# RWKV-5 attention with a SiLU MLP on one core: k turned by DMA in two 16-bit planes from unit 10 on

## The chip, the core and the metric

One core of a Trainium2 chip runs the kernel. Its engines are TensorE (PE in the profile, PEld for its weight loads), VectorE (DVE), ScalarE (ACT), GpSimd (POOL) and SyncE (SP), which here only issues DMAs. Each engine runs its own list of instructions in order and waits on semaphores. The metric is the device time of one execution in microseconds, the median of several runs.

## What is computed

For each of 4 batches and 8 heads a state of 48 x 48 runs over 768 steps, and the result goes through an MLP:

```python
for t in range(S):
    cur = np.einsum('bhd,bhe->bhde', u[None] * kt, vt)
    y[:, :, t] = np.einsum('bhd,bhde->bhe', rt, state + cur)
    state = w[None, :, :, None] * state + np.einsum('bhd,bhe->bhde', kt, vt)
...
h = x @ w_in                       # x: 3072 x 384, w_in: 384 x 2048
g = h * (1.0 / (1.0 + np.exp(-h)))
return (g @ w_out)                 # w_out: 2048 x 384
```

Inputs and output are f32.

## The kernel before

The sequence is cut into 6 chunks of 128 steps. A unit is one chunk of one batch with all 8 heads: unit i is chunk i//4 of batch i%4, 24 in all. Units 0 to 5 are done in an order written out by hand (the string `order`); the loop at L686 takes the others in pairs, i = 6, 8, ..., 22, where b = i%4 is 2 or 0. Tiles hold the time step on partitions, except for those that end in T, which hold the head's 48 channels there, two heads beside each other (partitions 0 to 47 and 64 to 111), in 4 groups.

A chunk is treated as two halves of 64 steps. Within a half the products of r and k are weighted by powers of w: r by w^t (`lamR`), k by w^-(t+1) (`lamK`). A pair i goes through these steps, each an engine's work:

- `sums` (L418, PE): k (weighted to the end of its half, `kc`, f16) times v, per half, into PSUM `sp`; `state_first` and `state_second` (L435, L449, DVE) add them to the decayed state (`sdec`, `st`). `spread_state` copies the state to f16 for the outputs (`s1h` on ACT, `s0h` on POOL and ACT).
- `product_halves` (L395, PE): kT times rT into PSUM `att`; `masked_halves` (L402, DVE) masks it into `am`.
- `outputs_halves` (L492, L501, PE): r times state and `am` times v into `yp`; `evict_halves` (L343, DVE) adds the bonus `vu` and gives `y16`; `turn_y_dma` (L524) turns y16 to `xT` by DMA transpose on SP's queue, one DMA for each unit.
- For the next pair (`nxt`, units i+2 and i+3): `bonus_products` (L223, L228, POOL) and `decayed_k` (L231, POOL, `kc`), `bonus_sum` (L236, DVE), `bonus_v` (L241, POOL), `cast_v` (L246, ACT, `v16`), `turn` (L255, PE: r and k of a unit turned in 64x64 blocks against an identity, 8 matmuls each, into `att`), `decay` (L270, DVE: rT and kT, times lamR and lamK), `decay_r16` (L270 and `rX`: the crossed halves of r in f16, on DVE or, where b=0, on ACT at L289).
- `load` (L72, SP): r, k, v of units i+4 and i+5, as r k v r k v, into rings of 8 buffers.

Between these, `fill(n)` takes n steps of the MLP from a list: an l1 step is 3 matmuls of 512 columns (L546) with xT as the moving operand and a SiLU on ACT (L555, `gT`); an l2 step is 4 matmuls (L568) with gT as weights, and each fourth of them ends a unit's output, which ACT copies to `osb` (L574) and SP stores (L578). A chunk has 16 of each. PSUM has four shared buffers (tag `moe`) for sp, yp, hps and ops, so a matmul that opens a new one waits until the engine that reads the oldest is done with it.

Of the kernel before, what the change touches and what calls it, by code (L numbers as in the profile page):

```python
# [7 lines left out]

FP = mybir.dt.float32
F16 = mybir.dt.float16  # L10
AF = mybir.ActivationFunctionType
ALU = mybir.AluOpType

# [2 lines left out]
def kernel(  # L16
# [33 lines left out]
    def unit(i):  # L50
        return divmod(i, B)
# [46 lines left out]

    RZ = 96
    w_row = cst.tile([RZ + 1, HD], FP)  # L100
    u_row = cst.tile([RZ + 1, HD], FP)
    ones = cst.tile([RZ + 1, 128], FP)
    idle = cst.tile([128, 512], F16)
    nc.scalar.preload_act_table_set("natural_log_exp_and_others")
# [6 lines left out]
    it_row = cst.tile([PR, 2, C], FP)  # L111
    it_rev = cst.tile([128, 1], FP)
    it_half = cst.tile([128, 1], FP)
    maskM = cst.tile([128, C], FP)
    maskH = cst.tile([128, HC], FP)
    ident16 = cst.tile([128, 128], F16)
    carry_pairs = [big.tile([PR, 2, NP, PW], F16, name=f"s0p{n}") for n in range(2)]
    inner_pairs = [big.tile([PR, 2, NP, PW], F16, name=f"s1p{n}") for n in range(2)]
    carry = [big.tile([D, 2, H, D], F16, name=f"s0h{n}") for n in range(3)]
    inner = [big.tile([PR, 2, H, D], F16, name=f"s1h{n}") for n in range(2)]  # L120

# [4 lines left out]
    def column_numbers():  # L126
        nc.gpsimd.iota(it_rev, pattern=[[0, 1]], base=C - 1, channel_multiplier=-1,
                       allow_small_or_imprecise_dtypes=True)
        for y in range(2):
            nc.gpsimd.iota(it_half[HC * y:HC * y + HC], pattern=[[0, 1]], base=HC - 1,  # L130
                           channel_multiplier=-1, allow_small_or_imprecise_dtypes=True)

    def mask():
# [17 lines left out]
    lnw_bc = cst.tile([128, HD], FP)  # L151
    lamC = cst.tile([128, H, D], FP)
    lamH = cst.tile([128, H, D], FP)
    wHT = cst.tile([PR, NP], FP)

    def pad(i, eng=nc.vector):
        for dst in (rin, kin):
# [32 lines left out]
    def spread_row(name, src):  # L190
        spread[name] = ps.tile([128, HD], FP, name="bc", tag="moe", bufs=4)
        nc.tensor.matmul(spread[name], ones, src, start=True, stop=True)
# [11 lines left out]
    def powers_h():  # L204
        nc.scalar.activation(out=lamH.rearrange("p h d -> p (h d)"), in_=lnw_bc,
                             func=AF.Exp, scale=it_half)
        nc.scalar.activation(out=wHT, in_=lnwT, func=AF.Exp, scale=float(HC))

    def silu_table():
        nc.scalar.preload_act_table_set("silu_and_others")  # L210

# [2 lines left out]
    def L(i):  # L214
        return live.setdefault(i, {})
# [14 lines left out]
    def decayed_k(i, eng=nc.gpsimd):  # L230
        eng.tensor_tensor(out=kc[i % NIN][:, :, 0:D], in0=kin[i % NIN][:, :, 0:D],  # L231
                          in1=lamH if in_halves(i) else lamC, op=ALU.mult)
# [8 lines left out]
        eng.tensor_tensor(out=L(i)["vu"], in0=vin[i % NIN],  # L241
                          in1=L(i)["rku"].unsqueeze(2).broadcast_to([128, H, D]), op=ALU.mult)

    def cast_v(i):
        L(i)["v16"] = wrk.tile([128, H, D], F16, name="v16", bufs=4)
        nc.scalar.copy(out=L(i)["v16"], in_=vin[i % NIN])  # L246

    def turn_one(i, x):
        if x == 0:
            L(i)["t"] = next_att().rearrange("p y (x g t) -> p y x g t", x=2, g=NP)  # L250
        flat = (rin, kin)[x][i % NIN].rearrange("p h d -> p (h d)")
        for p in range(NP):
            for y in range(2):
                rows = slice(HC * y, HC * y + HC)
                nc.tensor.transpose(L(i)["t"][0:PR, y, x, p, :], flat[rows, 128 * p:128 * p + PR],  # L255
                                    ident[rows, rows])
# [3 lines left out]

    def decay_one(i, x, key=None):
        lam = (lamR, lamK)[x]
        if key is None:
            key = "rk"[x] + "T"
            L(i)[key] = wrk.tile([PR, NP, C], FP, name=key)
        else:
            L(i)[key] = wrk.tile([PR, NP, C], F16, name=key, bufs=4)
        lam = (lam[:, :, 0:HC].unsqueeze(1).broadcast_to([PR, 2, NP, HC]) if in_halves(i)
               else lam.rearrange("p g (y t) -> p y g t", y=2))
        nc.vector.tensor_tensor(  # L270
            out=L(i)[key].rearrange("p g (y t) -> p y g t", y=2),
            in0=L(i)["t"][0:PR, :, x], in1=lam, op=ALU.mult)

    def early(i):
        return unit(i)[0] < 2
# [4 lines left out]
    def decay_r16(i, by_vector):  # L280
        decay_one(i, 0, "rT16")
        rx = L(i)["rX16"] = wrk.tile([PR, NP, HC], F16, name="rX16", bufs=4)
        for x in range(2):
            here, there = crossed_rows(x)
            if by_vector:
                nc.vector.tensor_tensor(out=rx[here], in0=L(i)["t"][there, x, 0],
                                        in1=lamR[there, :, 0:HC], op=ALU.mult)
            else:
                nc.scalar.copy(out=rx[here], in_=L(i)["rT16"][there, :, HC * x:HC * x + HC])  # L289

# [3 lines left out]

    def turn(i):
        turn_one(i, 0)
        turn_one(i, 1)

    def decay(i):
        decay_one(i, 0)  # L300
# [42 lines left out]
        nc.vector.tensor_tensor(out=y16[a], in0=y[b, 0:HD], in1=vu[a], op=ALU.add)  # L343

    def new_y(i):
        L(i)["y16"] = wrk.tile([128, H, D], F16, name="y16", bufs=4)

    def evict_first(i):
        new_y(i)
# [57 lines left out]
    def sums(i):  # L407
        sc, b = unit(i)
        xs = range(2 if sc < NCH - 1 else 1)
        L(i)["sp"] = [ps.tile([128, 512], FP, name="sp", tag="moe", bufs=4) for _ in xs]  # L410
        for p in range(NP):
            for e in range(2):
                for x in xs:
                    rows = slice(HC * x, HC * x + HC)
                    for j in range(2):
                        h = 2 * p + j
                        c0 = (e * NP + p) * D
                        nc.tensor.matmul(L(i)["sp"][x][64 * j:64 * j + 64, c0:c0 + D],  # L418
                                         kc[(i + e) % NIN][rows, h, :],
                                         L(i + e)["v16"][rows, h, :],  # L420
                                         start=True, stop=True)
# [94 lines left out]

    def x_tile(sc):
        if sc not in xts:
            xts[sc] = wrk.tile([128, NQ, B, C], F16, name="xT", bufs=2)
        return xts[sc]  # L520

    def turn_y_dma(i):
        sc, b = unit(i)
        nc.sync.dma_start_transpose(out=x_tile(sc)[:, :, b, :],  # L524
                                    in_=L(i)["y16"].rearrange("p h d -> p (h d)"))

    def turn_y(i):
        yf = L(i)["y16"].rearrange("p h d -> p (h d)")
# [3 lines left out]

    def copy_x(i, copy=nc.scalar.copy):
        sc, b = unit(i)
        copy(out=x_tile(sc)[:, :, b, :], in_=L(i)["yT"])

    gts = {}

# [2 lines left out]
    def l1_mm(sc, b0, nb, ft):  # L541
        m = B // nb
        hps = hpss[b0, ft] = ps.tile([128, m, nb * C], FP, name="hps", tag="moe", bufs=4)
        for f in range(m):
            for q in range(NQ):
                nc.tensor.matmul(hps[:, f, :], win[(ft + f) // 4].rearrange("p q (t c) -> p q t c", c=4)  # L546
                                 [:, q, :, (ft + f) % 4],
                                 xts[sc][:, q, b0:b0 + nb, :].rearrange("p b t -> p (b t)"),
                                 start=(q == 0), stop=(q == NQ - 1))

    def l1_silu(sc, b0, nb, ft):
# [76 lines left out]
    def piece(word, f):  # L628
# [7 lines left out]
        "wr": lambda: row(w_row, w), "wx": lambda: columns(nc.sync, wpT, w, 1),  # L636
        "wy": lambda: columns(nc.scalar, wpT, w, 0), "lnw": powers_r, "eK": exponents_k,
        "lamK": powers_k, "uc": copy_u, "wb": lambda: spread_row("w", w_row),
        "ub": lambda: spread_row("u", u_row), "lnwb": ln_w, "lamC": powers_c, "lamH": powers_h,
        "tab": silu_table, "clear": clear, "spin": lambda: None, "H": lambda: halved.pop(0)(),  # L640
    }
    unit_steps = {
# [16 lines left out]
        id16 lr1 pd3 lr3 lk3 clear 6*spin lv0 cg0 lv1 kz7 lr2 ak2 ku0 lv3 lr5 kz2 lv2 ub pd1 lv4  # L659
        lr4 lk4 lv5 pd2 lk5 lk7 lr6 lk6 uc T0 1*spin T1 lr7 lv7 kT0 pa4 rT0 ru0 ku1  # L660
        v160 pd5 lv6 rT1 kz6 rd0 kT1 wb ru1 P0 n0 2*spin rd1 P1 vu0 lnwb T2 n1 v161 2*spin
        pd7 lamC lamH pa6 i_q0 V0 v162 tab rT2 e0 kT2 ku2 T3 1*spin yT0 V1 kz5 vu1 i_q1 ru2
        xTD0 e1 P2 yT1 kT3 rd2 rT3 ku3 xTD1 P3 ru3 n2 rd3 v163 n3 L0.0 vu2 kc0 1*spin G0.0
        vu3 V2 L0.2 V3 G0.2 L0.4 e2 i_q2 e3 kc1 yT2 yT3 S0 G0.4 xT2 xTD3 kc2 L0.6 L2.4 G0.6
        st0 L2.0 scA0 v164 kc3 L2.6 ku4 i_q3 v165 L2.2 T4 rT4 kT4 G2.4 ru4 G2.2 T5 G2.0 G2.6
# [17 lines left out]
            unit_steps[word[:-1]](int(word[-1]))  # L683
    fillers.extend(halved + begun)

    for i in range(B + 2, NU, 2):  # L686
        sc, b = unit(i)
        nxt = range(i + 2, min(i + 4, NU))
        sums(i)
        product_halves(i)  # L690
        state_first(i)
        state_second(i)
        masked_halves(i)
        if i == B + 2:
            bonus_sum(i + 1)
            bonus_v(i + 1)
        for n in nxt:
            bonus_products(n)
            decayed_k(n)
        if i > B + 2 or sc < NCH - 1:  # L700
            next_state(i)
        fill(4)
        outputs_halves(i)
        next_crossed(i)
        for n in nxt:
            turn(n)
        evict_halves(i)
        turn_y_dma(i)
        turn_y_dma(i + 1)
        if b:  # L710
            fillers.extend((first(sc) if sc > 1 else rest_first(sc)) + second(sc))
        for n in nxt:
            decay(n)
        load(i + B)
        load(i + 1 + B)
        fill(4)
        for n in nxt:
            bonus_sum(n)
            cast_v(n)
            bonus_v(n)  # L720
        for n in nxt:
            fill(2)
            decay_r16(n, b)
        fill(4 if i < NU - 4 else 2)
    fill(len(fillers))


# [28 lines left out]
```

## Time and profile before

| | us |
|---|---|
| median of 3 runs | 187.34 (186.94 to 188.56) |
| the profiled execution | 186.19 |
| its span, first to last instruction | 184.5 |
| DMA queue of SP (q1), share of 16 engines | 50.3% |
| granted clock of TensorE | 0.998 |

The span is what the profile covers; the rest of the execution's time lies around it. A row of the profile names line, engine, operation, and output <- inputs; a matmul's own length in such rows overlaps its neighbours', so the cost of a run of them is read from the chain of waits, where each piece is counted until the next begins. A number in square brackets is idle time ahead of an instruction, with what ended it. "SPq" is the time for which SP's sequencer issued a DMA; the data land later.

### The profile page before, as it was taken

What the parts mean: (1) busy time and instruction counts of PE and PEld (TensorE: products, weight loads), DVE (VectorE), ACT (ScalarE), POOL (GpSimd) and SP (SyncE); (2) the same over time, 40 slices, a digit from 0 to 9 for tenths busy, and PEclk for the clock granted to TensorE, in tenths of its full rate; (3) what the DMA queues carried; (4) which work ended last, traced back from release to release, by engine and by line L of the source; (5) the groups of instructions that cost most, each with busy time, mean ns of one, the idle gap of its engine ahead of it and who ended that gap; (6) DMA issues with size and microseconds to landing.
All of it is one profiled execution on the core that took longest, in us unless ns stands there. A gap on an engine that the chain in (4) does not pass through costs nothing.

```text
span 184.5 us, 6822 instructions
## 1 busy us (share of the span) xinstructions
PE 177.5 (96%) x2913; PEld 117.2 (64%) x2913; DVE 115.9 (63%) x226; ACT 106.8 (58%) x209; POOL 112.1 (61%) x148
## 2 busy tenths in 40 slices
PE   7987998999999999999999999999999999999993
PEld 2565785688666976756657656657656566555563
DVE  4799729786885855895845985946974954000120
ACT  3462788599124694268694268694377692299200
POOL 7999999997999439639558567579169030000000
PEclk9999999999999999999999999999999999999999
DMA  5999999899596386386295396293396201410022
GB/s 95 235 211 210 167 216 195 151 221 230 100 190 198 89 168 138 87 171 174 46 176 130 87 182 163 48 217 88 87 187 159 46 4 49 125 43 0 0 88 85
DMA packets 88594, 24.24 MB, mean 131 GB/s; under 512 B 83314, under 2 KB 88052, under 8 KB 88564
## 3 DMA queue, kind: packets, MB, share of 16 engines
q1 hardware_dynamic: 83952, 20.19, 50.3%
q0 software_dynamic: 2176, 3.15, 10.2%
q10 hardware_dynamic: 2436, 0.46, 1.3%
q8 instruction: 23, 0.38, 0.8%
q14 instruction: 7, 0.06, 0.1%
HBM read 20.45 MB, written 4.72 MB: 136 GB/s over the span
## 4 chain that ended last, share of the span: by engine, by line
PE 73%; POOL 17%; DMA 6%; issue 2%; ACT 0%; POOLq 0%
PE ops L568 33%; PE hps L546 26%; DMA kin<-in_k_dram 6%; PE att L395 4%; PE att L255 4%; POOL ku L223 4%; POOL kc L231 3%; POOL rku_f L228 3%; POOL vu L241 2%; PE yp L492 2%; PE sp L418 2%; PE ops L593 1%; POOL win L83 1%; PE yp L501 1%; POOL wout L88 1%
## 5 line engine op out<-in xcount | busy, mean ns | idle before, releaser
L546 PE MATMUL hps<-xT,win 128*128 128x512 f16 (+1 forms) x360 | 66.3, 337 | 0.3 <-DMA win<-in_moe_w_in_dram 0.3
L555 ACT ACTIVATE gT<-hps 128x512 f16<-128x512 f32 x96 | 56.0, 597 | 14.1 <-PE hps L546 10.6
L568 PE MATMUL ops<-wout,gT 128*128 128x384 f16 x368 | 62.5, 326 | 0.0
L546 PEld LDWEIGHTS <-win 128*128 128x128 f16 x360 | 38.9, 114 | 21.3 <-DMA win<-in_moe_w_in_dram 0.4
L568 PEld LDWEIGHTS <-gT 128*128 128x128 f16 x368 | 35.2, 98 | 23.3
L241 POOL TENSOR_TENSOR vu<-vin,rku 128x384 f32<-128x384 f32 x24 | 19.6, 831 | 22.7 <-DVE rku L236 22.6
L223 POOL TENSOR_TENSOR ku<-kin,rin 128x384 f32<-128x384 f32 x24 | 24.1, 1003 | 11.6 <-DMA kin<-in_k_dram 11.5
L270 DVE TENSOR_TENSOR rT<-att,lamR 112x512 f32<-112x512 f32 (+1 forms) x40 | 26.9, 682 | 4.2 <-PE att L255 3.8
L574 ACT COPY osb<-ops 128x384 f32<-128x384 f32 x20 | 9.6, 479 | 34.1 <-issue 18.1
L343 DVE TENSOR_TENSOR y<-yp,vu 64x384 f16<-64x384 f32 (+1 forms) x34 | 18.9, 555 | 16.1 <-PE yp L501 8.0
L228 POOL TENSOR_TENSOR rku_f<-ku,u_bc 128x384 f32<-128x384 f32 x24 | 24.1, 1003 | 1.5
L231 POOL TENSOR_TENSOR kc<-kin,lamH 128x384 f16<-128x384 f32 x20 | 20.1, 1007 | 0.0
L270 DVE TENSOR_TENSOR kT<-att,lamK 112x512 f32<-112x512 f32 x24 | 16.3, 681 | 0.1
L246 ACT CAST v<-vin 128x384 f16<-128x384 f32 x24 | 11.3, 510 | 7.8 <-DMA vin<-in_v_dram 7.5
L435 DVE TENSOR_TENSOR s<-sp,sdec 112x384 f32<-112x384 f32 x10 | 5.6, 558 | 16.1 <-PE sp L418 16.1
L576 DVE COPY osb<-ops 128x384 f32<-128x384 f32 x3 | 1.7, 558 | 21.3 <-PE ops L568 21.3
L402 DVE TENSOR_TENSOR am<-att,maskH 128x1024 f16<-128x1024 f32 x10 | 12.2, 1219 | 1.1 <-PE att L395 1.1
L236 DVE TENSOR_REDUCE rku<-rku_f 128x8 f32<-128x384 f32 x24 | 12.4, 543 | 0.0
L395 PE MATMUL att<-rT,kT 48*64 48x64 f32 x640 | 11.9, 220 | 0.5 <-issue 0.5
L374 ACT CAST s1h<-s 48x384 f16<-48x384 f32 x16 | 8.1, 509 | 5.4 <-DVE s L435 5.2
L395 PEld LDWEIGHTS att<-rT,kT 48*64 48x64 f32 x640 | 10.6, 135 | 0.7 <-issue 0.7
L255 PE MATMUL att<-ident,rin 64*112 64x64 f32 x192 | 10.0, 223 | 0.4 <-DVE rku L236 0.4
(92 smaller groups left out, 175.0 us busy)
## 6 DMA issues: line engine op xcount, KB each, us to landing
rin<-in_r_dram SPq DMA_DIRECT2D x24, 192.0 KB, 3.9
vin<-in_v_dram SPq DMA_DIRECT2D x24, 192.0 KB, 4.3
out_dram<-osb SPq DMA_DIRECT2D x23, 192.0 KB, 2.7
kin<-in_k_dram SPq DMA_DIRECT2D x22, 192.0 KB, 4.5
win<-in_moe_w_in_dram POOLq DMA_DIRECT2D x4, 384.0 KB, 6.0
wout<-in_moe_w_out_dram POOLq DMA_DIRECT2D x4, 384.0 KB, 6.7
kin<-in_k_dram ACTq DMA_DIRECT2D x2, 192.0 KB, 3.7
xT<-y SPq DMA_TRANSPOSE x18, 2.3
```

The costliest lines, as they stand in the source:

```text
L223: eng.tensor_tensor(out=L(i)["ku"], in0=kin[i % NIN][:, :, 0:D], in1=rin[i % NIN][:, :, 0:D], op=ALU.mult)
L228: eng.tensor_tensor(out=L(i)["rku_f"], in0=L(i)["ku"], in1=u_bc, op=ALU.mult)
L231: eng.tensor_tensor(out=kc[i % NIN][:, :, 0:D], in0=kin[i % NIN][:, :, 0:D], in1=lamH if in_halves(i) else lamC, op=ALU.mult)
L236: nc.vector.tensor_reduce(out=L(i)["rku"], in_=L(i)["rku_f"], axis=mybir.AxisListType.X, op=ALU.add)
L241: eng.tensor_tensor(out=L(i)["vu"], in0=vin[i % NIN], in1=L(i)["rku"].unsqueeze(2).broadcast_to([128, H, D]), op=ALU.mult)
L255: nc.tensor.transpose(L(i)["t"][0:PR, y, x, p, :], flat[rows, 128 * p:128 * p + PR], ident[rows, rows])
L270: nc.vector.tensor_tensor(out=L(i)[key].rearrange("p g (y t) -> p y g t", y=2), in0=L(i)["t"][0:PR, :, x], in1=lam, op=ALU.mult)
L343: nc.vector.tensor_tensor(out=y16[a], in0=y[b, 0:HD], in1=vu[a], op=ALU.add)
L395: nc.tensor.matmul(a[o0:o0 + HC, j, e, p, :], kT[r0:r0 + D, p, HC * x:HC * x + HC], rT[r0:r0 + D, p, HC * x:HC * x + HC], start=True, stop ...
L546: nc.tensor.matmul(hps[:, f, :], win[(ft + f) // 4].rearrange("p q (t c) -> p q t c", c=4) [:, q, :, (ft + f) % 4], xts[sc][:, q, b0:b0 + ...
L555: nc.scalar.activation(out=gts[sc][:, ft:ft + m, b0 * C:(b0 + nb) * C], in_=hpss[b0, ft], func=AF.Silu)
L568: nc.tensor.matmul(opss[b], gts[sc][:, ft, b * C:(b + 1) * C], wout[:, ft, :], start=(ft == 0), stop=(ft == NFT - 1))
```

## The change

From unit 10 on (`by_planes`: i > 9) k is no longer turned on PE. POOL weights k by the channel's power of w relative to the middle of its half (`lamN`) into an f32 tile `kd`; a copy splits the f32 words of two units into their low and high 16-bit halves (`planes`, 128 x 2 x 2 x 8 x 64, zero in the padding); one DMA transpose on SP's queue turns both units' planes, 16 blocks of 128 x 128, into `turned`; and a copy on ACT joins the halves to f32 words again, `kT`. The sums' operand `kc` is now a cast of kd, on ACT where b=2 and on POOL where b=0, and v16 goes with it. r is weighted from the middle too (`lamS`, `lamM`), and the state is rescaled once, on POOL in i=6 and i=8, and then kept in that scale. `weighted_k` and `split_k` are done for units i+4 and i+5 in iteration i, right behind their loads, which now come as k k r r v v; the first split (units 10, 11) is on ACT in i=8. `masked_halves` moves ahead of `state_second`; `rX` is on DVE in every iteration; the two y16 of a pair lie in one tile and are turned by one DMA (6 blocks), for which xT has the unit ahead of the 128-channel block; the number of l2 steps ahead of the outputs is 3 for 4 where b=2.

```diff
+    it_mid = cst.tile([128, 1], FP)
-    carry_pairs = [big.tile([PR, 2, NP, PW], F16, name=f"s0p{n}") for n in range(2)]
-    inner_pairs = [big.tile([PR, 2, NP, PW], F16, name=f"s1p{n}") for n in range(2)]
+    blocks16 = big.tile([128, 8 * NP * PW], F16)
...
+    kd = [lnw_bc, u_wide]
+    lamM = lamR[:, :, HC // 2:HC // 2 + HC]
+    turned = blocks16[:, 0:16 * C].bitcast(U16).rearrange("p (e y g t) -> p e y g t", e=2, y=2, t=C)
+    lamN = cst.tile([128, H, D], FP)
+    lamS = cst.tile([PR, NP, HC], FP)
+    planes = big.tile([128, 2, 2, H, 64], U16)
...
+    def powers_n():
+        nc.scalar.activation(out=lamN.rearrange("p h d -> p (h d)"), in_=lnw_bc,
+                             func=AF.Exp, scale=it_mid)
...
     def decay_one(i, x, key=None):
         lam = (lamR, lamK)[x]
+        if by_planes(i):
+            lam = lamS if key is None else lamM
...
+    def clear_planes():
+        nc.gpsimd.memset(planes.rearrange("p e y h d -> p (e y h d)").bitcast(F16), 0.0)
+
+    def by_planes(i):
+        return i > 2 * B + 1
+
+    def powers_s():
+        nc.gpsimd.tensor_tensor(out=lamS, in0=lamR[:, :, 0:HC],
+                                in1=lamK[:, :, HC // 2 - 1:HC // 2].broadcast_to([PR, NP, HC]), op=ALU.mult)
+
+    def rescale_state(i):
+        t = st[unit(i)[1] // 2]
+        nc.gpsimd.tensor_tensor(
+            out=t, in0=t, in1=lamK[:, :, HC // 2 - 1:HC // 2].unsqueeze(1).broadcast_to([PR, 2, NP, D]),
+            op=ALU.mult)
+
+    def cast_k(i, copy=nc.scalar.copy):
+        copy(out=kc[i % NIN][:, :, 0:D], in_=kd[i % 2].rearrange("p (h d) -> p h d", h=H))
+
+    def weighted_k(i):
+        nc.gpsimd.tensor_tensor(out=kd[i % 2].rearrange("p (h d) -> p h d", h=H), in0=kin[i % NIN][:, :, 0:D], in1=lamN, op=ALU.mult)
+
+    def split_k(i, copy=nc.gpsimd.tensor_copy):
+        copy(out=planes[:, i % 2, :, :, 0:D],
+             in_=kd[i % 2].bitcast(U16).rearrange("p (h d y) -> p y h d", h=H, y=2))
+
+    def turn_planes():
+        nc.sync.dma_start_transpose(out=turned.rearrange("p e y g t -> p (e y g) t"),
+                                    in_=planes.rearrange("p e y h d -> p (e y h d)"))
+
+    def join_k(i):
+        L(i)["kT"] = wrk.tile([PR, NP, C], FP, name="kT")
+        nc.scalar.copy(
+            out=L(i)["kT"].rearrange("p g t -> p (g t)").bitcast(U16)
+            .rearrange("p (n y) -> p n y", y=2),
+            in_=turned[0:PR, i % 2].rearrange("p y g t -> p (g t) y"))
...
     def turn(i):
         turn_one(i, 0)
-        turn_one(i, 1)
+        if not by_planes(i):
+            turn_one(i, 1)
...
-            xts[sc] = wrk.tile([128, NQ, B, C], F16, name="xT", bufs=2)
+            xts[sc] = wrk.tile([128, B, NQ, C], F16, name="xT", bufs=2)
...
-        nc.sync.dma_start_transpose(out=x_tile(sc)[:, :, b, :],
-                                    in_=L(i)["y16"].rearrange("p h d -> p (h d)"))
+        nc.sync.dma_start_transpose(out=x_tile(sc)[:, b:b + 2].rearrange("p b q t -> p (b q) t"),
+                                    in_=L(i)["yy"].rearrange("p e h d -> p (e h d)"))
...
-                                 xts[sc][:, q, b0:b0 + nb, :].rearrange("p b t -> p (b t)"),
+                                 xts[sc][:, b0:b0 + nb, q, :],
...
+    clear_planes()
+    powers_s()
     for i in range(B + 2, NU, 2):
         sc, b = unit(i)
         nxt = range(i + 2, min(i + 4, NU))
+        after = range(i + 4, min(i + 6, NU))
+        split = i + 2 < NU and by_planes(i + 2)
         sums(i)
         product_halves(i)
         state_first(i)
+        masked_halves(i)
         state_second(i)
-        masked_halves(i)
+        if by_planes(i + 4) and not by_planes(i):
+            rescale_state(i)
         if i == B + 2:
             bonus_sum(i + 1)
             bonus_v(i + 1)
+        if i == 2 * B:
+            for n in nxt:
+                split_k(n, nc.scalar.copy)
+        if split:
+            turn_planes()
+        if b and split:
+            for n in nxt:
+                cast_k(n)
+                cast_v(n)
         for n in nxt:
             bonus_products(n)
-            decayed_k(n)
+            if not split:
+                decayed_k(n)
         if i > B + 2 or sc < NCH - 1:
             next_state(i)
-        fill(4)
+        if not b and split:
+            for n in nxt:
+                cast_k(n, nc.gpsimd.tensor_copy)
+                cast_v(n, nc.gpsimd.tensor_copy)
+        fill(3 if b and split else 4)
         outputs_halves(i)
         next_crossed(i)
         for n in nxt:
             turn(n)
         evict_halves(i)
         turn_y_dma(i)
-        turn_y_dma(i + 1)
         if b:
             fillers.extend((first(sc) if sc > 1 else rest_first(sc)) + second(sc))
         for n in nxt:
-            decay(n)
-        load(i + B)
-        load(i + 1 + B)
+            if split:
+                decay_one(n, 0)
+                if b:
+                    join_k(n)
+            else:
+                decay(n)
+        for dst, src in ((kin, k), (rin, r), (vin, v)):
+            for n in after:
+                ld(n, dst, src)
         fill(4)
+        if i > 2 * B and not b and split:
+            for n in nxt:
+                join_k(n)
         for n in nxt:
             bonus_sum(n)
-            cast_v(n)
+            if not split:
+                cast_v(n)
             bonus_v(n)
+        for n in after:
+            weighted_k(n)
+        if after and by_planes(i + 4) and not i == B + 2:
+            for n in after:
+                split_k(n)
         for n in nxt:
             fill(2)
-            decay_r16(n, b)
-        fill(4 if i < NU - 4 else 2)
+            decay_r16(n, True)
+        if i == 2 * B and split:
+            for n in nxt:
+                join_k(n)
+        fill((5 if b and split else 4) if i < NU - 4 else 2)
```

## The prediction

> **What bounds it now.** I read the page's busy shares first, then the chain of waits in order of time, then the timelines of SP, ACT and POOL in one iteration.
>
> ```profile
> PE 177.5 (96%) x2913; PEld 117.2 (64%) x2913; DVE 115.9 (63%) x226; ACT 106.8 (58%) x209; POOL 112.1 (61%) x148
> 83.29 0.37 PE sp L418 x32
> 83.66 0.98 PE att L395 x63
> 84.64 2.71 PE hps L546 x12
> 87.36 0.37 PE yp L492 x32
> 87.73 0.28 PE yp L501 x32
> 88.01 1.04 PE att L255 x32
> 89.05 4.66 PE hps L546 x21
> 93.70 3.25 PE ops L568 x20
> 96.95 0.37 PE sp L418 x32
> ```
>
> Columns are start, length, what. This is all of the iteration i=12, 13.66 us, and each piece starts where the one before ends: from 47.6 us to the end the chain is TensorE alone. So an instruction taken off PE there is worth its time, as long as nothing else comes late. I write +x for x us after an iteration's first sums matmul.
>
> SP's queue, ACT, and rows of POOL and ACT by form:
>
> ```profile
> 88.71 2.48 SPq L524 DMA_TRANSPOSE xT<-y  x2
> 91.28 0.53 SPq L72 DMA_DIRECT2D rin<-in_r_dram  x1
> 91.91 0.53 SPq L72 DMA_DIRECT2D kin<-in_k_dram  x1
> ```
>
> ```profile
> 89.85 2.54 ACT L555 ACTIVATE gT<-hps 128x512 f16<-128x512 f32 x4 [1.47 <-PE hps L546]
> 92.42 0.93 ACT L246 CAST v<-vin 128x384 f16<-128x384 f32 x2
> ...
> 95.19 0.60 ACT L555 ACTIVATE gT<-hps 128x512 f16<-128x512 f32 x1
> ```
>
> ```profile
> L228 POOL TENSOR_TENSOR rku_f<-ku,u_bc 128x384 f32<-128x384 f32 x24 | 24.1, 1003 | 1.5
> ...
> L374 POOL CAST s0h<-st 48x384 f16<-48x384 f32 x8 | 4.0, 499 | 0.0
> ```
>
> ```profile
> L289 ACT COPY rX<-rT 48x256 f16<-48x256 f16 x16 | 6.4, 403 | 0.3
> ```
>
> The first fence shows SP issuing: one DMA transpose of 3 blocks of 128x128 holds the queue 1.2 us, a load 0.53. The gT lines show how little room ScalarE has: the last gT ends at 95.79 and the l2 matmul that needs it comes 15 x 0.1625 us (3.25/20) after 93.70, at 96.14: 0.35 us of slack. The last two are prices (busy us, mean ns).
>
> **Removed from PE.** In iterations 8, 10, ..., 20 the 16 k transposes of two units: half of the 1.04 us, 0.52 x 7 = 3.64 us. The iteration becomes 13.1 us. The two kT products on DVE go too (2 x 0.68); DVE takes rX back where b=0 (4 x 0.42). It waited 1.1 to 3.0 us for the sums each time, so this ends on no path. am moves ahead of the four st updates: PE gets am 1 us sooner, st comes 1.2 us later, and its readers on POOL stand behind 4 us of bonus products.
>
> **xT in another order.** The l1 matmuls read four runs of 128 in place of one of 512. No row has that. 42 matmuls of 256 columns took 4.71 us (112 ns), 21 of 512 took 4.66 (222 ns): a joint costs 2 ns at most, three joints in 192 matmuls at most 1.3 us; I take 0, as the price goes by columns; a gain is excluded, since no column is saved.
>
> **The transpose of the planes.** 16 blocks a pair. The trace has 3 blocks in 1.2 us of queue. Bounds: 1.2 us (all fixed) and 16/3 x 1.2 = 6.4 (all by blocks). I take a load's 0.53 as the fixed part, (1.2 - 0.53)/3 = 0.22 a block: P = 4.0 us, and 1.8 for the new y pair (6 blocks, 2.4 before). A y transpose lands 2.3 us from issue, 1.1 after its queue time, so the planes land P + 1.1 = 5.1 us after their issue.
>
> The Trainium skill's Advanced Engine Details and Errata, "X-Bar Transpose (TRN2)", says such transposes are as fast as regular DMAs; by that, half a megabyte at its 350 GB/s would be an estimated 1.5 us. The trace disagrees as far as it goes: the 98 KB ran at 205 to 224 GB/s, and only once 1.1 us of issue had gone by.
>
> **ACT.** Each join is a copy of 112x1024. From 403 ns for 256 elements and 620 for 512 (L306) the slope is 0.85 ns, so 1.06 us each; bounds 0.93 (gT's slope from 597) and twice that if two bytes at a stride cost double. Two are 2.1 us. In b=0 iterations they stand where v16 (0.93) and partly rX (1.62) were: four gT end at +8.6, joins to +10.7, three gT to +12.6, while PE, 0.52 earlier, wants the last at +12.33: it waits 0.3, in i=12, 16, 20: 0.9 us. In b=1 iterations (10, 14, 18) the join waits at the head of ACT for the planes, and behind it stand two osb and five gT. PE's hps need those PSUM buffers: the next sums take the buffer of the third gT, joins + 2.9 us, at +12.9. So joins have to end by +10.0, planes to land by +7.9.
>
> **POOL.** The kc products (2 x 1.0) become weighted_k (the same), two splits and, for b=0, four casts (0.5 each, as s0h). The split copies 768 two-byte elements: the slope of POOL's casts, 292 ns for 128 and 499 for 384, gives 0.81 us; the other end is the tensor_tensor's 2.6 ns an element, 2.0 us. I take 0.81, the nearer operation. Per iteration: ku, rku 4.0, s0h and sdec 1.3, vu 1.6, weighted 2.0, splits 1.6 and casts 2.0: 12.5 of 13.1 us (b=0), 10.5 (b=1). It fits, barely. Ahead of the loop: memset of the planes 1.9 (739 ns for 768), lamS 0.7, st 0.8 in i=6; vu of unit 7 is thereby 2 us late, with 7.9 us of l2 matmuls to cover. Two iota at the start, 0.26 us, and lamN, 0.6 on ACT ahead of 4.0 us of idle: nothing, 0.3 at most, where PE already waits 0.6 for kin at 47.5.
>
> **The new ring.** SP issues planes, y, then loads with k first. POOL waits in the same iteration for these k (before, they were wanted an iteration later), splits, and SP's next planes wait for that; stores, y and six loads are queued behind. Length: P 4.0 + a store (0.6 every second time: 0.3) + y 1.8 + both k landed and weighted. The first load of a burst lands 2.9 us after issue, the second 4.0 to 5.4 after the first's issue (3.4 to 4.8 after its own): I take 4.6, + 1.0 for the second product + 1.6 for splits + 0.1 = 7.3. Sum 13.4 us against the 13.1 us iteration: it runs level, 0.3 late each time. Iteration 8: POOL gets to weighted_k(11) by 59.0, ACT splits (0.84 each) to 59.9, so planes go at 59.9. k of 12 at 66.4, split to 73.6, which is +4.5 in i=10: land +9.6, joined +11.8, PE stalls 1.8. Then by the same steps planes start at +3.3, 3.0, 3.4, 3.2, 3.5 in i=12 to 20: PE stalls 0.2 and 0.4 in 14 and 18, the 0.3 in b=0.
>
> **Sum.** -3.64 + 1.8 + 0.2 + 0.4 + 0.9 = -0.3 us with these values. With k landing at the short end (4.0) the ring is 12.8, i=10 stalls 1.2 and the others not: -1.5. I take the middle, -0.9: span 183.6; with the 1.69 us around the span (186.19 - 184.5) 185.3; the profiled execution was 1.15 below the median of 187.34, so 186.4 us.
>
> **Rivals.**
> 1. *The turn is cheap and the gain stays.* If issue is nearly fixed, P = 1.2 and the landing is bounded by moving: 16 blocks at the y's 0.16 us of all engines are 2.5 us, so 4.3. y then waits for its eviction, not for SP; planes go at +3.4 in i=10, joined at +9.8, no stall; only b=0's 0.9 or none is left: -2.7 to -3.6, 183.7 to 184.6. For it: DMA is at 60% over an iteration, and 2.5 us more of 13.1 are free. Against: 1.2 us of issue for 98 KB. The skill's rule above, in Advanced Engine Details and Errata, would end here.
> 2. *The ring sets the pace (slower).* The ring is P + y + 7.6; once P + y passes some 5.8 us every further tenth is paid in each turn. At the far end (P 6.4, y 2.4) it is 16.4 a turn: planes(20) at 59.9 + 6 x 16.4 = 158.3, joined 9.6 later (landing 7.5, joins 2.1), 167.9, where product(22) was at 150.5: +17.4, 204.7. At P = 5 (y 2.1) the ring is 14.7: 59.9 + 88.2 = 148.1, joined 8.2 later at 156.3: +6, 193. For it: it starts level in my own sum. Against: it needs a block at 0.3 us, where the split of a load's issue says 0.22.
> 3. *POOL's split is dear.* At 1.4 us each, midway, the ring is 14.6 and POOL in b=0 13.7: planes(20) at 147.5, joined 7.2 later, 154.7: +4.2, 191.5. For it: POOL's tensor_tensor at 2.6 ns an element. Against: its casts at 0.8.
> That PE still turns k can be left out: the changed program has 8 transposes less per unit.
>
> **Chances.** Measured against no change, 1% (1.87 us) is about what can be told. Forecast case (185.4 to 188): 0.35. Rival 1: 0.36. Rival 2: 0.17. Rival 3: 0.12. Faster by over 1%, below 185.47: rival 1 and a little of the forecast, 0.38. Within 1%: 0.34. Slower, over 189.2: 0.28. The range leaves out the far half of rivals 2 and 3 and the last tenth of rival 1: 183.7 to 191.5; the forecast case's own is 185.4 to 188.
>
> **What would show it.** DMA_TRANSPOSE of the planes on SP's timeline: 4.0 us (1.2 for rival 1, 5 and more for rival 2), landing 5.1. The joins at 1.06 us each. The splits on POOL at 0.8 (rival 3: 1.4 and up). L255 in the chain 0.52 long from i=8 on, the distance of sums 13.1 to 13.4 us from i=12 on and some 15 in i=10. PE waiting for ACT in the b=1 iterations means late planes; POOL waiting for kin ahead of weighted_k says that the ring is taut. Wrong would be: l1 matmuls longer than 222 ns, or PE stalls ahead of 55 us.

## The result, and the profile after

| | before | after |
|---|---|---|
| median of 20 runs each, us | 186.95 (185.75 to 188.56) | 185.8 (183.63 to 187.24) |
| the profiled execution, its span | 186.19, 184.5 | 185.0, 183.3 |
| first sums matmul of i=8 | 55.94 | 56.91 |
| from there to the end of the span | 128.56 | 126.39 |

The ratio is 0.9915, with an interval of 0.9887 to 0.9943: about 1.6 us faster. It compares fast runs only, those within 1.5% of the fastest of their kernel, which leaves out five of the twenty after and one of the twenty before; the medians of all runs differ by 1.15 us. In the stretch that the change touches the two traces differ by 2.17 us; 0.97 of it is hidden in this pair of traces by a later start of i=8, which the last section takes up.

The busy shares on the first part of the page after the change:

```profile
PE 174.3 (95%) x2801; PEld 113.8 (62%) x2801; DVE 114.8 (63%) x228; ACT 115.6 (63%) x208; POOL 132.3 (72%) x182
```

PE has 112 transposes less, POOL 20 us more work, ACT 9. The chain of waits in order of time, the same iteration i=12:

```profile
83.46 0.37 PE sp L477 x32
83.83 0.98 PE att L454 x63
84.81 2.71 PE hps L605 x12
87.53 0.37 PE yp L551 x32
87.89 0.28 PE yp L560 x32
88.18 0.59 PE att L272 x16
88.77 4.66 PE hps L605 x21
93.43 2.44 PE ops L627 x15
95.86 0.03 issue
95.89 0.99 PE ops L627 x5
96.88 0.37 PE sp L477 x32
```

Two rows differ from before. The transposes (L272, L255 before) take 0.59 for 1.04: 0.45 saved. The 20 l2 matmuls, 3.25 before, are now split 15 and 5, with 0.03 of "issue" between and 0.99 where 5/20 of 3.25 is 0.81: 0.2 us lost. PE's weight loads say for what: over the loop they have this row (line, what they waited for, us in total, times, longest):

```profile
PEld L627 <- ACT gT L614: 0.8, 2, 0.4
```

That is the last gT, behind the two joins on ACT, in i=12 and 16. From one sums(i) to the next the trace after has 13.26, 13.29, 13.42, 13.55, 13.41, 13.17 and 11.87 us, that before 13.71, 13.64, 13.66, 13.64, 13.66, 13.62 and 12.31. So 0.45 is gained in i=8, 18 and 20, and 0.09 to 0.35 in i=10 to 16, where something waits.

SP's timeline (start, us for which SP was held, what) around i=10 and 12:

```profile
60.96 3.00 SPq L320 DMA_TRANSPOSE blocks<-planes  x1
...
73.62 1.34 SPq L320 DMA_TRANSPOSE blocks<-planes  x1
75.57 0.98 SPq L637 DMA_DIRECT2D out_dram<-osb  x1
76.64 1.25 SPq L583 DMA_TRANSPOSE xT<-y  x1
77.95 1.19 SPq L73 DMA_DIRECT2D kin<-in_k_dram  x2
...
84.92 3.26 SPq L320 DMA_TRANSPOSE blocks<-planes  x1
90.07 1.21 SPq L583 DMA_TRANSPOSE xT<-y  x1
```

The rows of the planes' DMA by its tile (ns min/median/max, first and last start), and from issue to landing:

```profile
L320 SPq DMA_TRANSPOSE blocks<-planes x7: 1336/2686/3257, 61.0 to 138.6; - x7
...
DMA to landing us min/median/max: 4.5/5.0/6.8
```

Sixteen blocks hold SP for 1.34 us where the queue is empty, six for 1.21 to 1.25, three for 1.19 before: the issue goes by the DMA, not by its blocks. In the iterations with b=0 the same DMA holds SP for 2.7 to 3.3 us, and in i=14 and 18 for 1.49 and 2.17. Stores and loads issued before it may be the reason; no run isolates it. And the copies, from the groups by form:

```profile
L325 ACT COPY kT<-blocks 112x1024 uint16<-112x1024 uint16 x14 | 15.6, 1161 | 5.6 <-DMA blocks<-planes 5.5
...
L316 POOL COPY planes<-u_wide 128x768 uint16<-128x768 uint16 x6 | 4.9, 824 | 0.0
```

ACT waits 5.5 us in all for the planes (in i=10, 14, 18), but PE hardly sees it.

### The profile page after: what moved, and what is told of

It is laid out like the page before. It is cut to its first block, busy times and chain, and to the rows that moved or that the text cites. A ratio compares the mean times of both kernels' runs of the same rounds, so it can differ in the third digit from the quotient of the medians.

```text
span 183.3 us, 6609 instructions
## 1 busy us (share of the span) xinstructions
PE 174.3 (95%) x2801; PEld 113.8 (62%) x2801; DVE 114.8 (63%) x228; ACT 115.6 (63%) x208; POOL 132.3 (72%) x182
## 3 DMA queue, kind: packets, MB, share of 16 engines
q0 software_dynamic: 2176, 3.15, 9.8%
## 4 chain that ended last, share of the span: by engine, by line
PE 86%; POOL 6%; DMA 4%; issue 2%; ACT 0%; POOLq 0%
PE hps L605 34%; PE ops L627 33%; PE att L454 6%; PE att L272 4%; DMA win<-in_moe_w_in_dram 4%; PE sp L477 2%; PE yp L551 2%; PE yp L560 2%; PE ops L652 1%; POOL ku L240 1%; POOL rku_f L245 1%; POOL vu L258 1%; POOL kc L713 1%; POOL blocks L152 1%; PE yp L543 1%
## 5 line engine op out<-in xcount | busy, mean ns | idle before, releaser
L614 ACT ACTIVATE gT<-hps 128x512 f16<-128x512 f32 x96 | 55.2, 598 | 12.4 <-PE hps L605 9.3
L289 DVE TENSOR_TENSOR rT<-att,lamR 112x512 f16<-112x512 f32 (+1 forms) x26 | 17.7, 681 | 4.1 <-PE att L272 3.8
L325 ACT COPY kT<-blocks 112x1024 uint16<-112x1024 uint16 x14 | 15.6, 1161 | 5.6 <-DMA blocks<-planes 5.5
L342 DVE TENSOR_TENSOR rX<-att,lamR 48x256 f16<-48x256 f32 x32 | 13.5, 421 | 0.5
L263 ACT CAST v<-vin 128x384 f16<-128x384 f32 x16 | 7.9, 509 | 9.1 <-DMA vin<-in_v_dram 9.0
L313 POOL TENSOR_TENSOR lnw_bc<-kin,lamN 128x384 f32<-128x384 f32 x7 | 7.0, 997 | 6.4 <-DMA kin<-in_k_dram 3.6
```

The lines of the kernel that those rows point to most:

```text
L289: nc.vector.tensor_tensor(out=L(i)[key].rearrange("p g (y t) -> p y g t", y=2), in0=L(i)["t"][0:PR, :, x], in1=lam, op=ALU.mult)
L325: nc.scalar.copy(out=L(i)["kT"].rearrange("p g t -> p (g t)").bitcast(U16) .rearrange("p (n y) -> p n y", y=2), in_=turned[0:PR, i % 2].re ...
L614: nc.scalar.activation(out=gts[sc][:, ft:ft + m, b0 * C:(b0 + nb) * C], in_=hpss[b0, ft], func=AF.Silu)
```

## The experiments

Theory: the whole gain is PE's, 0.45 us in each of seven iterations; planes, joins and splits run beside PE, and what is given back are short waits behind ACT and SP. Rivals: the gain comes from another edit (order of loads, am ahead, one y DMA a pair); the turn by DMA costs something that the wait lists don't show; the ring of planes, y and loads has no room. Each edit below is against the changed kernel, and each ratio against runs of the kernel before on the same chip.

**k also on PE.** The turned k is written and not used.

```diff
-        if not by_planes(i):
-            turn_one(i, 1)
+        turn_one(i, 1)
```

> The changed kernel, with the 16 k transposes of a pair put back on PE beside the planes (their result is not used). If the gain is PE's time alone: 16 more matmuls in 7 iterations, 0.45 us each (1.04 in the chain before, 0.59 for r alone after), 3.2 us over the changed kernel, so about 189 us, 1% over the kernel before. If the gain comes from the other parts (one y transpose a pair, k loaded first, am ahead of st, rX on DVE), it stays at about 0.99 of before.

Measured: 187.73 us, ratio 1.0037 (1.001 to 1.0063). From sums(8) to the end 129.5 us for the 126.39 of the changed kernel: 3.1 given back. The time is 0.4% over the kernel before, not the 1% expected, since the loop of the kernel before takes 128.56. The chain's row for the transposes is as it was before the change:

```profile
88.60 1.04 PE att L272 x31
```

**All but the planes**, with PE turning k as before the change.

```diff
     def by_planes(i):
-        return i > 2 * B + 1
+        return False
...
-    clear_planes()
-    powers_s()
...
-        if i == 2 * B:
-            for n in nxt:
-                split_k(n, nc.scalar.copy)
...
-        for n in after:
-            weighted_k(n)
```

> The changed kernel without the planes: k turned on PE in every unit and weighted as before, no weighted_k, split, join or rescaling; the other parts stay (xT's order, one y transpose a pair, loads k k r r v v, am ahead of st, rX on DVE). If the gain is the k turn on PE: about the time before, ratio 0.995 to 1.005. If the other parts carry it: 0.99. If they cost something that the planes pay for: over 1.005.

Measured: 187.15 us, 1.001 (0.9976 to 1.0043); from sums(8) to the end 128.6, before 128.56. So the order of the loads, am ahead of st, the layout of xT and one y DMA for two are worth nothing here by themselves. These two runs settle where the gain is from: PE's transposes, 7 x 0.45 = 3.15.

**The join on DVE.**

```diff
-        nc.scalar.copy(
+        nc.vector.tensor_copy(
```

> The two joins of an iteration on DVE in place of ACT. If the last gT behind the joins is what costs 0.2 us in i=12 and 16 and the queue behind the joins what costs 0.1 in i=10: these go, 0.5 us faster than the changed kernel, ratio to before about 0.989. Rival: DVE then waits for the planes at the head of its own queue, with bonus_sum and rT16 behind it, and POOL's vu behind those: 0.5 to 2 us slower than the changed kernel, 0.995 to 1.0.

Measured: 189.04 us (186.59 to 194.54), 1.0076 (1.0034 to 1.0119), much the widest spread of all. The trace is of a long execution, 191.36 us; two of the twelve took 186.59 and 186.9, so what it shows need not be in each. In it the time is lost in one place, and not to the planes. DVE's timeline, then POOL's, at the end of i=8:

```profile
68.34 7.29 DVE L325 COPY kT<-blocks 112x1024 uint16<-112x1024 uint16 x2
```

```profile
72.70 0.99 POOL L240 TENSOR_TENSOR ku<-kin,rin 128x384 f32<-128x384 f32 x1
73.76 1.32 POOL L245 TENSOR_TENSOR rku_f<-ku,u_bc 128x384 f32<-128x384 f32 x1
75.05 1.45 POOL L240 TENSOR_TENSOR ku<-kin,rin 128x384 f32<-128x384 f32 x1
```

The planes were issued at 59.9 and landed 5.9 us later at most; the two copies began at 68.34 and took 5.89 and 1.48 us. The median of the 14 is 0.69, on ACT 1.16. POOL ran one instruction after another from 59.7 to 77.6, and when the copies at last got through, two of POOL's took 0.3 and 0.45 us more than their 1.0. The other twelve copies took 0.68 to 1.56, the long ones again beside POOL's work. PE waited 4.6 and 0.9 us for kT. From 74 to 80 us, behind the long wait, the granted clock was 0.50, and the products and the l2 matmuls that followed took 5.6 us where the changed kernel's take 3.0. So i=8 and 10 together last 34.52 us for 26.55: the waits are 5.5 of it and the slower clock some 2.5. From i=12 on this trace has no wait on PE: 13.22, 13.20, 13.21, 13.17 and 11.86 us from one sums to the next, 0.76 less in all than the changed kernel. There the waits for gT are gone, as expected. The Trainium skill's SBUF — State Buffer, "SBUF: two separate sides", says that DVE and GpSimd share a pair of ports as a lock: a DVE operation in a two-port mode and a GpSimd operation exclude each other for a whole instruction. The trace fits that, as copies and POOL's instructions took longer where they met. The first copy took 5.2 us more than the median, the time of several POOL instructions in a row and not of one. That the port is the cause is read from this coincidence; no run took POOL's work away from beside the copies.

**Both joins behind the last gT where b=0.**

```diff
-        if i > 2 * B and not b and split:
-            for n in nxt:
-                join_k(n)
...
-        if i == 2 * B and split:
+        if not b and split:
```

> In i=12, 16, 20 the joins stand behind all gT of the iteration, as they do in i=8 already. If PE's wait ahead of the last five l2 matmuls is for the gT behind the joins: it is gone from the chain (0.2 us twice), 0.4 us faster than the changed kernel, ratio 0.989. Rival: the joins end after the next sums and product_halves waits for kT instead: no change or up to 1 us slower.

Measured: 186.01 us, 0.9929 (0.9894 to 0.9964), from sums(8) to the end 127.1. The gT wait is gone (the 20 l2 matmuls take 3.25 in one piece), but the last pair's kT comes late, as PE's timeline shows:

```profile
150.15 1.04 PE L454 MATMUL att<-rT,kT 48*64 48x64 f32 x56 [0.47 <-ACT kT L325]
```

One wait for another; the two ends of ACT's slack are about one join apart. PE's weight loads also wait for xT, 0.3 us in i=10 and 0.6 in i=18.

**One join on each side of the three gT.**

```diff
-            for n in nxt:
-                join_k(n)
+            join_k(i + 2)
...
-        if i == 2 * B and split:
-            for n in nxt:
+        if not b and split:
+            for n in nxt if i == 2 * B else (i + 3,):
```

> In i=12, 16, 20 one of the two joins stays ahead of the last three gT and the other goes behind them. If ACT's order there is what PE waits for: the five l2 matmuls at the iteration's end take 0.81 us again, not 0.99 with 0.03 of waiting ahead, and no wait for kT comes in its place (second join over by +12.7 us after the iteration's first sums matmul, wanted at +13.4): 0.4 us faster than the changed kernel over the loop. Rival: kT late, as with both joins behind (PE waited 0.5 us for kT there): no change. Ratio to before 0.989 to 0.992 either way; the chain decides.

Measured: 185.44 us, 0.9893 (0.9834 to 0.9951). Neither the wait for gT nor the one for kT is left. The trace itself, of one of its longer runs, takes 128.25 us from sums(8) to the end, 1.86 more than the changed kernel's: PE waits 0.65 for xT in i=10, and 0.47 and 0.84 for nothing that the profile shows.

**POOL splits each k twice.**

```diff
             for n in after:
                 split_k(n)
+                split_k(n)
```

> POOL's splits done twice (1.64 us more in each iteration, same output). If the ring (planes, y, loads of k, weighting, split, planes) had no room, as the prediction had it: each iteration 1.6 us longer from i=10 on, 8 us in all, about 194. If it has room of some 2 us (planes were issued at +1.2 to 1.6 us of the iteration, and y waited for its eviction, not for SP): only the planes of i=10 come too late (now at +3.4, joins over at +10.8): 1 to 2 us more than the changed kernel, about 187 to 188.

Measured: 188.62 us, 1.0095 (1.006 to 1.0131), some 3 us slower than the changed kernel, not 1 to 2; from sums(8) to the end 129.98, 3.6 more. What comes late is not kT. SP's timeline, then PE's, in i=10:

```profile
76.16 1.32 SPq L320 DMA_TRANSPOSE blocks<-planes  x1
77.57 1.26 SPq L637 DMA_DIRECT2D out_dram<-osb  x1
78.92 1.26 SPq L583 DMA_TRANSPOSE xT<-y  x1
```

```profile
82.67 3.43 PE L605 MATMUL hps<-xT,win 128*128 128x512 f16 x15 [2.42 <-DMA xT<-y]
```

Planes stand ahead of y in SP's queue, and behind late planes y is late; the 5.9 us of l2 matmuls and transposes that cover the way from y to xT don't suffice then. A second such wait, 1.15 us, is in i=14; there y needed 4.98 us to land, 2.8 of median without this edit. The two make 3.57 of the 3.6 us.

**Early work on DVE:** the memset of the planes and lamS.

```diff
-        nc.gpsimd.memset(planes
+        nc.vector.memset(planes
...
-        nc.gpsimd.tensor_tensor(out=lamS,
+        nc.vector.tensor_tensor(out=lamS,
...
-        st0 L2.0 scA0 v164
+        st0 L2.0 scA0 pl lamS v164
...
-    clear_planes()
-    powers_s()
```

> The planes' memset (1.79 us) and lamS (0.61) move from POOL in i=6 to DVE in the hand-ordered start. If POOL's lateness there costs (planes of i=8 go at 61.0, those of i=10 at +3.4): planes 2 us sooner, 0.1 to 0.5 us faster than the changed kernel. If PE's list alone sets the pace up to i=10: no change.

Measured: 185.31 us, 0.9871 (0.9821 to 0.9922), not told apart from the change alone. The trace is of the longest of its six runs, 187.78 us. The planes went at +3.67 in i=8 (4.05 without the edit) and at +3.46 in i=10, as without it. In i=8 they don't wait for POOL: its second weighted k was done at 58.59 us, but the splits of units 10 and 11 stand on ACT behind the two s1h of i=8, which wait for this iteration's sums, and so ran only from 60.07 to 61.64. In the changed kernel the same: POOL done at 59.71, the splits from 59.37 to 60.94 behind s1h. The place of the splits on ACT sets the first planes.

**The kernel before, once more**, for its start.

> The kernel before, once more, for a second profile: whether the first sums of i=6 and i=8 (41.6 and 55.9 us in its first profile; 41.2 to 43.3 and 56.1 to 57.2 in five changed ones) vary by themselves. If the start is random: 41 to 43 here too. If the change made it later: 41.6 and 55.9 again. From the sums of i=8 to the end 128.6 us either way.

Measured: 186.69 us, one run; sums(8) at 56.22, 128.68 from there to the end. So the start moved by 0.28 us without a change, less than the 0.97 between the two traces above.

**The planes' DMA alone**, added to the kernel without planes (e2 in the expectation; the edit is against that one): the transposes carry zeros and nothing reads them.

```diff
+    clear_planes()
...
-        if split:
+        if i + 2 < NU and i >= 2 * B:
             turn_planes()
```

> The kernel of e2 (k turned on PE, no splits, no joins) with the planes' DMA transpose of zeros added in each iteration from i=8 on; its result is not used. In the three profiles without it (before twice, e2) PE waited nowhere after 50 us; in those with it PE waited at odd places for nothing that the profile shows (0.1 to 0.8 us) and for xT. If the DMA's traffic and its place in SP's queue make these waits: they show here too, 0.2 to 1.5 us over e2 (187.2), ratio 1.002 to 1.008. If the waits come from the work on POOL and ACT: none here, as e2.

Measured: 186.39 us, 0.9994 (0.9968 to 1.002); 128.87 from sums(8) to the end, and no wait on PE in the loop. So seven times 512 KB beside the loads slow nothing by themselves. With no splits to wait for, these DMAs go at +0.3 to +2.0 and y is on time; late planes are not tested here.

**The store behind y where b=2.**

```diff
-        nc.sync.dma_start(out=out[tt:tt + C, :], in_=osb)
+        held.append(lambda: nc.sync.dma_start(out=out[tt:tt + C, :], in_=osb))
+        if not hold:
+            held.pop()()
...
+        hold.extend([0] if b and split else [])
         fill(3 if b and split else 4)
+        hold.clear()
...
         turn_y_dma(i)
+        while held:
+            held.pop(0)()
```

> The changed kernel; where b=2, the store that SP issues between the planes and the y transpose goes behind the y transpose. If the first l1 matmuls of these iterations wait for xT because y stands behind planes and store: y 0.5 to 1 us sooner, no PE wait for xT, 0.1 to 0.6 us faster than the changed kernel. Rival: y waits for its eviction anyway: no change, the wait stays.

Measured: 184.22 us, 0.9878 (0.9847 to 0.9908), beside 184.59 for the changed kernel on this chip (below), with overlapping intervals; and its trace, 126.87 from sums(8) to the end, is longer than the changed kernel's 126.41. A gain isn't shown. No wait for xT is left. In its place PE loses 0.28 us in i=10 to the joins, by way of PSUM; the chain:

```profile
78.92 1.16 ACT kT L325
80.07 0.39 ACT osb L633
80.46 0.04 issue
80.50 2.10 PE hps L605 x9
```

The joins ended at +11.2, osb stood behind them, and the next hps needed the buffer that osb empties.

**The three together** (one join each side, early work on DVE, store behind y).

> e5's join on each side, e7's early work on DVE and e10's store together. If each takes away a wait of its own: about 1 us faster than the changed kernel, ratio to before 0.985 to 0.988. If they only move one wait to another place: 0.99 to 0.992, as the changed kernel.

**The changed kernel again**, beside it.

> The changed kernel beside these on the same chip: ratio 0.99 to 0.993. In the first profile the loop, from the sums of i=8 to the end, took 126.4 us for 128.6 before. If the waits for code and for xT come and go: 126 to 128 here, with PE waits of 0.1 to 1 us at places other than in the first profile.

| same chip | median, us | ratio | sums(8) to the end |
|---|---|---|---|
| changed kernel | 184.59 (184.13 to 184.93) | 0.9897 (0.9865 to 0.9929) | 126.41 |
| three together | 184.24 (183.22 to 184.7) | 0.9868 (0.9831 to 0.9905) | 125.95 |

In the trace of the three together the two l2 pieces of i=12 are one again (3.25), and PE's wait list holds neither gT, osb, xT nor kT. The trace is 0.46 us shorter, about half of what was expected; the medians differ by 0.35 with overlapping intervals, so that this version beats the changed kernel isn't shown by its times. It beats the kernel before.

## Why the prediction was right, and where its steps were off

The forecast was 186.4 us and the range 183.7 to 191.5; 185.8 came. The sign of the sum and its main term held, but two terms in it were off and made up for each other in part: the saving was put too high and the waits too high as well. That the time came so near is partly luck. The loop gained 2.27 us, outside the sum's own 0.3 to 1.5 and between it and rival 1's 2.7 to 3.6, and the mechanism was rival 1's: a cheap turn, no ring that sets the pace. In the two traces what brought the time back towards the forecast lies ahead of the loop: i=8 starts 0.97 us later, where the prediction had "nothing, 0.3 at most".

- **Removed from PE.** Put at 0.52 x 7 = 3.64, half of the 1.04; measured 0.45 x 7 = 3.15. The 16 transposes that are left take 0.59: between 0.59 for 16 and 1.04 for 32 the slope is 0.028 us each, and 0.14 don't go by number. Half a row's time is not the cost of half its instructions.
- **xT's layout.** Taken as 0 of at most 1.3 us: 21 l1 matmuls take 4.66 us in both traces, and all but the planes costs nothing.
- **P, the queue time of the planes.** This is the step that failed: 4.0 us, from a fixed 0.53 of a load and 0.22 a block. At its shortest it is 1.34, near the lower bound of 1.2, and the mean of the seven is 2.45; y's is 1.25 for the 1.8 predicted. Rival 1 had it. The 2.7 to 3.3 us in the b=0 iterations are nearer the predicted size but don't go by blocks (1.34 and 3.26 for the same DMA).
- **Landing.** 5.1 predicted, 5.0 median. Here the number was right with a wrong split: from 6 blocks (2.8) to 16 (5.0) it grows by 0.22 us a block, but not in the issue, since the planes of i=10 and i=8 landed after 5.0 and 4.9 us with issues of 1.34 and 3.00. A block is 32.8 KB, so if the growth is all moving it is 149 GB/s. It isn't fixed: in the run with the planes' DMA alone the median was 6.0. The rule weighed in the prediction, in the Trainium skill's Advanced Engine Details and Errata, "X-Bar Transpose (TRN2)", gives 350 to 400 GB/s; no run here showed that, nor the estimated 1.5 us worked out from it.
- **The i=10 stall of 1.2 to 1.8.** Planes predicted at +4.5, joins over at +11.8; they were at +3.45 and +10.8. ACT's timeline shows the joins waiting for the planes (square brackets) and done at 80.93:

```profile
78.70 2.23 ACT L325 COPY kT<-blocks 112x1024 uint16<-112x1024 uint16 x2 [2.62 <-DMA blocks<-planes]
80.83 0.85 ACT L633 COPY osb<-ops 128x384 f32<-128x384 f32 x2
```

  PE lost 0.1 us there, in an iteration with b=2 ("b=1" in the prediction). The mechanism, PSUM buffers behind the joins, exists: with joins over at +11.2, in the run with the store behind y, it cost 0.28. But the bound of +10.0 was too early, since +10.8 cost only 0.1; and in that run PE waited for the osb right behind the joins, not for a gT.
- **The ring.** Put at 13.4 us against 13.1, level. The part from k's issue to the end of the splits was right (7.3 predicted; 77.95 to 84.89 is 6.9), the planes' queue time was not: the turn from 73.62 to 84.92 is 11.3 us. Then it runs in step with PE, as y waits for its eviction: planes at +1.2 to +1.6 in i=12 to 20, for +3.0 to +3.5 predicted. So the ring had some 2 us a turn to spare where rival 2 needed it taut (and by rival 2's own P + y + 7.6 the limit at 13.1 us is 5.5 for P + y, not 5.8), and the stalls of 0.2 and 0.4 in i=14 and 18 for late kT didn't come.
- **Rival 3.** The split is 0.82 us, predicted 0.81: the row of the nearer operation was the right one. The price of the rival's case is known from the kernel that splits twice: 0.82 more for each split cost some 3 us, so the rival's 1.4 (0.58 more) would, as an estimate by proportion, have cost some 2 us, about what the change gains. Its forecast of +4.2 had the wrong victim: y behind the planes on SP, not kT.
- **ACT.** The join took 1.16 for 1.06, and the last gT waits 0.2 in i=12 and 16 for the 0.3 predicted in 12, 16 and 20. In i=20, which ends with 12 l2 matmuls and not 20, there is none.
- **Not priced.** y stands behind planes and a store on SP, and the l1 matmuls of b=2 iterations want xT. In the repeated run of the changed kernel PE loses 0.26 us in i=10: its weight loads wait 0.29 us for xT, and 0.27 more with no releaser shown, until 80.61, when the first osb behind the joins had ended at 80.56. So the loss belongs to both. The prediction counted every queue position for the planes' sake and not for y's.

Summed over the loop after the change: -3.15, +0.10 in i=10, +0.21 and +0.20 for gT in i=12 and 16, and +0.36 in i=14, of which 0.14 is shown as "issue" within the r transposes and nothing in the profile accounts for it: -2.28 us, where the intervals between sums show -2.27. The prediction's -0.3 to -1.5 took 2.1 to 3.3 us of waits where 0.87 came, and a saving larger by 0.49. The 2.27 of the loop and the 1.15 to 1.6 of the times aren't the same either; whether the change makes the start later on average is open.

## What to carry to other kernels

Where PE is busy without a gap, 3.2 us of its work were bought off with 29 us on POOL and ACT, which had the room; it needs each buffer's chain followed to its end: here the thin places were the order on ACT and what stands behind the new DMA on SP, not the DMA. Price half of a run of matmuls by a row that has half of them, not by halving. And an issue that was measured at one size of DMA should be bounded at "all fixed" before it is scaled by size.

## What the runs showed of the hardware

- A DMA transpose on a free SP queue was held 1.19 us for 3 blocks, 1.21 to 1.26 for 6, 1.32 to 1.36 for 16 at the shortest; the DMA of 16 blocks was also held for 1.4 to 3.6 us elsewhere, and for 4.22 (one join each side, i=12) and 4.37 (early work on DVE, i=12). What sets it is not isolated: 0.8 to 0.9 us behind a store it was held 1.33 (store behind y, i=18) and 2.75 (repeat of the changed kernel, i=14).
- A copy of 112x1024 uint16 took 0.69 us on DVE and 1.16 on ACT, but up to 5.89 on DVE while POOL ran without a pause.
- With the join on DVE a wait of PE of 4.6 us, 69.7 to 74.3, was followed by a granted clock of 0.50 from 74 to 80 us and about 1.0 after: the matmuls in that stretch took some 2.6 us more than in the changed kernel.
- In ten of fourteen traces PE stands idle before the same product matmuls at about 32 us, with no releaser shown; here the profile after, PE's timeline:

```profile
33.65 0.33 PE L454 MATMUL att<-rT,kT 48*64 48x64 f32 x3 [1.74 <-issue]
```

  It is 0.51 us in the profile before, 1.74 after, 0.89 in the repeat of the changed kernel and 1.25 with the planes' DMA alone. It differs between runs of one kernel, and so does the start of i=8 (55.99 in the repeat, 55.33 to 57.99 over all traces), which is why the loops are compared from sums(8) on. The two don't go together throughout: without this idle time i=8 began at 56.55 (one join each side) and 57.99 (early work on DVE). The clock has a part too: with both joins behind the last gT and with the split done twice the granted clock was 0.50 from 20 to 22 us, 1.00 in the other traces, and i=8 began at 57.18 and 57.02. Within the loop the turn of r in i=14 shows the like, always after 7 of 16 matmuls: 0.14 in the changed kernel, 0.84 with one join each side. No run shows what PE waits for there, and the cause stays open.
